# Issue order of the opening phase: pieces of the last chunk as they land, idle matmuls dropped, one v block loaded ahead of half of w_out, and new written-out orders for the first seventeen blocks

## The chip, the core and the metric

The kernel runs on one core of a Trainium2 chip. The metric is the device time of one execution in microseconds (us), the median over several runs. In profiles, PE is TensorE (matmuls), PEld its weight loads, DVE is VectorE, ACT is ScalarE, POOL is GpSimd, SP is SyncE; POOL, SP and ACT also issue DMAs.

## The reference

Cross-covariance attention over four batches, whose result goes through a two-layer MLP with a tanh GELU:

```
B, N, C = 4, 6080, 256
qn = q / (norm(q, axis=1) + 1e-6)          # columns over the 6080 tokens
kn = k / (norm(k, axis=1) + 1e-6)
s  = kn.transpose(0, 2, 1) @ qn / tau      # 256 x 256 for each batch
a  = softmax(s, axis=-1)
x  = (v @ a).reshape(24320, 256)
h  = x @ w_in                              # 256 -> 2048
g  = 0.5*h*(1 + tanh(sqrt(2/pi)*(h + 0.044715*h**3)))
out = g @ w_out                            # 2048 -> 256, float32
```

## The kernel before, in words

**Per batch.** The kernel never forms x. For each batch it sums the Gram matrix of q and k over the tokens (tile `G`) and the squares of their columns (tiles `ss`), makes the scores, their exponentials `eT` and row sums, and multiplies the attention matrix into w_in: `aw` = a·w_in, 256x2048 in bf16. The MLP then needs only v, transposed: h = v·aw.

**Per block.** The 24320 tokens are 48 blocks of 512 (the twelfth of each batch has 448). The transposed v of a block is the tile `vT`. For blocks 0 and 1, v comes into SBUF and TensorE transposes it (`load_v0`, `pe_vt`, copies by VectorE). From block 2 on, `cast_v(n)` has GpSimd issue a DMA that casts v to bf16 in DRAM (tile `vb`, line 152), and SyncE issues a transposing DMA from there (`load_vt`, line 162). A block's 16 column groups of h are made in 8 pairs. Pair p of block n is `g<p>`: four 512-wide matmuls into a two-bank PSUM tile, followed by ScalarE's GELU, `G<p>`. There are two such PSUM tiles, tags "h" and "b": in blocks 0 and 1, pairs 0, 2, 4, 6 use "h" and pairs 1, 3, 5, 7 use "b" (`SIDE`). A pair can only start when the GELU that reads the same tile is done. From block 2 on some pairs are made in sets by a scheme with fewer multiplications (`w0...`, `w1...`: matmuls `m1` to `m7`, ScalarE copies `cq`, `y5`, VectorE additions `ap`, `ax`, GELUs `Gq`, `Gr`, `Gx`).

**The second layer** is made by seven products per block, each in halves of four 256-wide matmuls (`M1A`, `M1B`, ... `M7B`). They read sums of g made by VectorE (`T1a` to `T4b`) and combinations of w_out (tile `wcomb`). Those combinations are prepared once, from the two halves of w_out (tiles `wst`, 1 MB each, `load_wout(0)` and `load_wout(1)`): `pA11` and `pS3` need the first half only, `pF0` is their first sum of both halves (line 660), `pS1`, `pF1`, `pS2`, `pS4` follow it. `M1` needs `pA11`, `M5` needs `pS1`, `M6` needs `pS2`. Results are turned by VectorE (`c11` to `c22`) and stored by SyncE's DMAs, four for a block.

**The opening.** Batch 0's q and k come in six chunks. The last chunk of 8 rows comes in five pieces, in the order q 0:4, k 0:5, k 5:8, q 4:6, q 6:8 (`PIECES`, tile `last`). For it, `square_rows` squares pieces on ScalarE (q 0:4) and VectorE (the others), `gram_row` adds Gram rows, `ss_rows(c, 1)` adds k's squares (256-wide matmuls against ones, line 274) and `ss_rows(c, 0)` adds q's (one-column matmuls, line 268). `warm(n)` issues n matmuls on zeros whose result nobody reads (line 369). `scores(0)` takes the sums to `eT`: logarithm and exponential on ScalarE for k's row factors (`lnk`, `rk`) and q's (`lnq`, `rq`), two products on VectorE (`S`), two exponentials on ScalarE. `first_aw` makes the first 512 columns of `aw`; the others are `aw2` to `aw7` (two 512-wide matmuls each, line 460) with a copy by VectorE (`ac2` to `ac7`, line 473). Pairs 2 and 3 need `ac2` and `ac3`; `aw6` writes the PSUM bank that `ac4` reads.

**Order.** Each engine runs its instructions in the order in which the program issues them. From block 0 on that order is written out by hand as strings of step names: `ORDER[WINDOW[n]]` lists the steps issued in the stretch of block n, and `x+1` or `x-1` is step x of the next or the previous block. `lt`, `lv`, `lq`, `lk` are DMA issues (`vT`, `vb`, q and k of a later batch). GpSimd's DMAs rotate over eight semaphores, so each waits until the eighth one before it has landed.

Of the kernel before, what the change touches and what calls it, by code (L numbers as in the profile page):

```python
# [18 lines left out]
def kernel(  # L19
# [962 lines left out]
    """g0 w0cq T3b-1 lt+2 w0y5 lv+3 row1-1 c11a-2 M4A-2 G0 T2b-1 w0m6 M5B-1 w0ap row3-1 ksq-1
    M4B-2 T2a-1 w0m2 w0m7 row0-1 w0ax w0m3 g3 w0Gq c21-2 lq+1 T3a-1 M5A-1 G3 M1B-1 T4a-1 M1A-1
    c22-2 w0Gx g4 SW1-2 y5-1 cq-1 g5 c11-2 G4 lt+3 lv+4 vs+1 w0m4 M6B-1 w0Gr M6A-1 qsq-1 g6
    ap-1 T1a lk+1 M3A-1 G6 row2-1 M3B-1 f1-1 w0m1+1 G5 M7A-1 T4b-1 w0m5+1 M7B-1 w0y5+1 c12-1
    row5-1 row3 ax-1 w0cq+1 row2 T2a row4-1 g7 ksq f2-1 w0m6+1 row0 w0ap+1 M4B-1 G7 M2A-1
    M2B-1 qsq M4A-1 c11a-1""",
    """g0 f3-2 c21-2 w0m7 G0 w0m2 T2b-1 w0m3 M5A-1 w0ax M1A-1 w0Gq T3a-1 g3 vs+1 w0Gx M1B-1 G3
    w0m4 f1-1 lq+1 M5B-1 g4 cq-1 c22-2 w0Gr w1m5 T1a G4 M6B-1 M6A-1 lt+3 lv+4 w1m1 y5-1 row1-1
    f2-1 w1cq g7 ap-1 w1y5 T4b-1 w1m6 G7 row5-1 w1ap M3A-1 lk+1 row4-1 T3b-1 M3B-1 qsq w0m5+1  # L990
    c12-1 w1m7 w1m2 w1ax w1m3 M7B-1 w1Gq T4a-1 M2A-1 w1m4 c11-2 M2B-1 w1Gr T2a M7A-1 w0y5+1
    row0 ax-1 w0m1+1 w1Gx""",
    """g0 c11a-2 w0cq T3b-1 M4A-2 G0 T3a-1 row5-1 w0m6 M4B-2 f3-2 ksq-1 row2-1 w0ap g3 c21-2
    T2b-1 w0m3 G3 w0m7 w0m2 w0ax M5B-1 lq+1 M1A-1 w0Gq T4a-1 M1B-1 f4-2 w0m4 cq-1 M5A-1 w0Gr
    f1-1 w1m5 M6A-1 y5-1 w1m1 M6B-1 f2-1 w1cq lt+3 lv+4 g4 ap-1 w1y5 c22-2 w0Gx w1m6 c11-2
    M3B-1 w1ap G4 M7B-1 vs+1 row3-1 M3A-1 qsq lk+1 w1m7 f3-1 g7 w1ax T4b-1 w1m3 G7 row4-1 w1m2
    c12-1 w1m4 row1-1 f4-1 M7A-1 w1Gr row2 w1Gq ax-1 M2A-1 T1a w0m1+1 w0m5+1 M2B-1 w0y5+1""",
    """g0 T2a-1 w0cq w1Gx-1 M4A-2 c11a-2 T4a-1 w0m6 G0 M4B-2 w0ap M5A-1 ksq-1 M5B-1 c22-2 c21-2
    row1-1 w0m2 vs+1 w0m7 w0m3 g3 w0Gq w0ax lq+1 T2b-1 M1B-1 G3 w0m4 c11-2 M1A-1 T3a-1 g4 w0Gr
    f1-1 cq-1 w1m5 G4 row4-1 M6A-1 lt+3 lv+4 T4b-1 w1m1 M6B-1 f2-1 y5-1 w1cq g7 ap-1 w1y5  # L1000
    T3b-1 w1m6 G7 M3A-1 w1ap lk+1 M3B-1 M7B-1 w0Gx c12-1 w1m7 ksq M7A-1 w1ax w1m3 w0m5+1 ax-1
    w1m2 w1m4 T1a M2A-1 w1Gr M2B-1 w1Gq row4 c11a-1 row3-1 w0m1+1 f3-1 row0-1 w0cq+1 M4B-1
    c11-1 M4A-1 w0y5+1 row5-1 qsq c21-1 w0m6+1""",
    """g0 w0ap f4-2 M5A-1 w1Gx-1 w0m3 c22-2 w0m7 G0 w0m2 w0ax row2-1 M1A-1 w0Gq T3a-1 M1B-1 w0m4
    T2a-1 g3 cq-1 T3b-1 w0Gr lq+1 M5B-1 G3 f1-1 g4 T2b-1 row0-1 G4 w1m1 M6A-1 T4a-1 w1m5 f2-1
    M6B-1 lt+3 lv+4 y5-1 w1cq g7 ap-1 w1y5 f3-1 w1m6 w0Gx row1-1 w1ap M3B-1 G7 M3A-1 vs+1 lk+1
    w1m7 w1m2 ksq row5-1 w1ax M7B-1 M7A-1 c12-1 T1a w1m3 w1m4 M2A-1 w1Gr M2B-1 ax-1 w1Gq
    w0m5+1 T4b-1 row3-1 w0m1+1 row1 c11a-1 w0cq+1 row0""",
    """g0 T2a-1 w0y5 c11-2 w1Gx-1 w0m6 M4B-2 w0ap G0 M4A-2 f4-2 row4-1 w0m3 qsq-1 w0m7 c22-2 g3
    w0ax w0m2 c21-2 G3 M5A-1 T2b-1 lq+1 w0m4 M1A-1 f1-1 w0Gr row3-1 M1B-1 w0Gq T4a-1 row5-1  # L1010
    w1m1 w1m5 T4b-1 cq-1 M5B-1 w1cq g4 f2-1 lt+3 lv+4 w1y5 T3a-1 w1m6 y5-1 M6A-1 G4 w1ap
    row2-1 M6B-1 f3-1 w0Gx w1m2 T3b-1 w1m3 w1m7 qsq lk+1 g7 ap-1 w1ax M7A-1 f4-1 G7 M3B-1 vs+1
    w1m4 M3A-1 w1Gr M7B-1 c12-1 w1Gq row1 ax-1 w0m5+1 w0m1+1 T1a M2A-1 w0cq+1 M2B-1 w1Gx""",
    """g0 c22-2 w0y5 c11a-2 row2-1 T3a-1 G0 w0m6 M4B-2 w0ap M5B-1 ksq-1 T2b-1 M4A-2 w0m7 c21-2 g3
    w0ax M1A-1 f1-1 G3 w0m2 w0m4 M1B-1 T2a-1 w0Gr w0m3 M5A-1 f2-1 cq-1 T3b-1 row4-1 w0Gq w1m5
    w1m1 c11-2 M6B-1 T4b-1 y5-1 M6A-1 w0Gx lt+3 lv+4 g4 ap-1 w1cq T4a-1 w1y5 M3A-1 f3-1 G4
    w1m6 M3B-1 w1ap row3-1 M7A-1 qsq c12-1 w1m3 vs+1 M7B-1 g7 ax-1 ksq T1a row4 row0 w1m7
    M4A-1 w1ax M2A-1 G7 f4-1 M2B-1 w1m4 c11a-1 row5-1 w1Gr w1m2 f1 M4B-1 w1Gq row1 row2 row0-1
    f2 row5 w0m5+1 f3 w0m1+1 T3a""",
    """lq+4 g0 w0cq c21-2 w0y5 M5B-1 T2a-1 G0 w0m6 M1A-1 w0ap M1B-1 w1Gx-1 f4-1 row3-1 w0m7 cq-1  # L1020
    g3 T2b-1 gc w0ax w0m3 G3 w0m2 M5A-1 T4a-1 w0m4 ss c11-2 w0Gr T3b-1 w0Gq w1m5 sv M6A-1
    T4b-1 pow w1m1 y5-1 M6B-1 c22-2 w1cq g4 lt+3 lv+4 ap-1 w1y5 vs+1 w1m6 G4 M7A-1 w1ap lk+4
    M7B-1 kf M3A-1 w0Gx ax-1 g7 kr T1a w1m7 G7 M3B-1 w1m3 c12-1 w1m2 krp w1ax w1Gq M4A-1 S1+1
    w0m5+1 w1m4 S0+1 w1Gx M2A-1 T2a w1Gr M2B-1 T3a w0y5+1 M4B-1 w0m1+1 th0+1 c21-1""",
    """g0 w0cq c22-2 c11a-2 th1 M1B-1 T3b-1 G0 M1A-1 T2b-1 w0m6 M5A-1 dn w0ap g3 cq-1 rc0 w0m7 G3
    w0m3 w0m2 w0ax M6B-1 lq+4 M5B-1 rc1 w0Gq w1m5 w0m4 M6A-1 rc2 w0Gr g4 y5-1 lt+3 lv+4 w1y5
    ap-1 w1m1 rc3 M3B-1 w1cq M3A-1 G4 vs+1 w1m6 M7B-1 w1ap w0Gx g7 c12-1 eT w1m7 G7 M2A-1 w1ax
    w1m3 w1m2 M7A-1 T4b-1 w1Gq M2B-1 T4a-1 lk+4 w1m4 rsum+1 ax-1 w0m5+1 w1Gr""",
    """g0 rs T1a-1 w0y5 w0m1 aw0 w0cq M4B-2 ac0 G0 M4A-2 c11-3 w0m6 aw1 w1Gx-1 w0ap g3 ac1 c21-2
    T2b-1 w0m7 w0m3 G3 aw2 w0ax M1B-1 c11a-2 w0Gx w0m2 ac2 w0m4 M1A-1 w0Gr T3b-1 M5B-1 w0Gq  # L1030
    w1m5 T2a-1 aw3 w1m1 cq-1 M5A-1 ac3 lt+3 lv+4 w1cq g4 vs+1 y5-1 w1y5 aw4 SW0 G4 M6B-1 w1m6
    M6A-1 ac4 w1ap g7 lq+4 ap-1 T3a-1 w1m7 aw5 c22-2 w1m2 w1m3 ac5 w1ax M7B-1 G7 T1a M3B-1
    M3A-1 w1Gx w1m4 w0m5+1 c12-1 w1Gr M7A-1 c11-2 aw6 w1Gq T4b-1 w0m1+1 M2B-1 ax-1 w0y5+1
    T4a-1 M2A-1 w0cq+1""",
    """g0 T2b-1 ac6-1 c11a-2 w0m6 G0 M4A-2 w0ap M4B-2 c22-2 aw7-1 c21-2 w0m7 g3 ac7-1 w0ax M1A-1
    G3 M1B-1 SW1-1 lk+3 w0m4 w0m2 cq-1 w0m3 T3b-1 M5A-1 w0Gr T2a-1 M6B-1 w0Gq M5B-1 vs+1 w1m1
    w1m5 y5-1 M6A-1 T3a-1 lt+3 lv+4 w1cq g4 ap-1 w1y5 T4a-1 w0Gx w1m6 M3B-1 w1ap G4 M7A-1
    M3A-1 c11-2 w1m2 c12-1 w1m3 w1m7 w1Gq g7 w1ax M7B-1 G7 w1m4 ax-1 M2A-1 T4b-1 M2B-1 w1Gr
    M4A-1 T1a w1Gx M4B-1 w0m5+1 w0m1+1 w0y5+1""",
    """g0 lq+3 c21-2 T3a-1 w0cq M1A-1 c11a-2 G0 T2a-1 w0m6 M1B-1 c22-2 M5A-1 ksq w0ap g3 T3b-1  # L1040
    w0m7 cq-1 row2 w0ax G3 row1 M5B-1 T2b-1 row3 w0m4 y5-1 w0m2 T4a-1 w0Gr w0m3 M6A-1 w0Gq
    c11-2 w1m5 w1m1 lt+3 lv+4 row4 M6B-1 w1cq g4 ap-1 w1y5 lk+3 T4b-1 w0Gx w1m6 M3A-1 G4 w1ap
    M7B-1 T1a M3B-1 qsq M7A-1 w1m2 ax-1 w1m3 w1m7 g7 w1Gq w1ax vs+1 M4B-1 G7 w1m4""",
    """g0 T2a-1 w1Gr-1 c22-2 M4A-2 w1Gx-1 c12-2 w0m5 T4a-1 w0m1 w0y5 M2B-2 c21-2 M2A-2 w0cq T3a-1
    row1 G0 row5 T3b-1 M1B-1 w0m6 c11a-2 M1A-1 ksq w0ap g3 lq+3 f1-1 w0m7 cq-1 M5B-1 w0ax G3
    row3 w0m3 T2b-1 w0m2 M5A-1 w0Gq row0-1 w0m4 lt+3 lv+4 M6B-1 w0Gr M6A-1 y5-1 w1m5 w1m1 w0Gx
    ap-1 g4 w1cq T4b-1 w1y5 M3A-1 vs+1 w1m6 G4 M7B-1 w1ap M3B-1 qsq f2-1 M7A-1 c11-2 w1m7 g7
    w1ax ax-1 row5-1 lk+3 G7 row0 f3-1 w1m4 w1m2 w1m3 c12-1 M4B-1 w1Gr c22-1 w0m5+1 f1 w1Gq
    M4A-1 w0m1+1 M2B-1 w0cq+1 f2 M2A-1 c21-1 w0y5+1""",
    """g0 T1a-1 w1Gx-1 w0m6 G0 M1A-1 w0ap M1B-1 c11a-2 row5 qsq w0m7 T2a-1 row1 g3 w0ax cq-1 w0m2  # L1050
# [171 lines left out]
```

## Time and profile before

| | |
|---|---|
| median of 5 runs (lowest to highest) | 698.01 us (697.73 to 698.22) |
| the profiled execution: its time / its span | 698.22 us / 696.4 us |
| PE, DVE, ACT, POOL busy, of the span | 96%, 90%, 89%, 10% |
| granted TensorE clock, mean | 0.997 |
| PE, its share of the chain that ended last | 92% |
| PE's first matmul / last wait for an input chunk ends / first matmul of block 0's pairs | 10.39 / 28.76 / 38.51 us |

The span runs from the first to the last instruction; the time is 1.82 us more. Times in the profile count from the span's start. A group line gives start, length, engine, source line, operation, output and inputs, and how many instructions are merged; the brackets give the idle time just before and what ended it. Ends of matmuls are modelled, and adjacent ones overlap; the time from one start to the next is what one takes of PE.

### The profile page before, as it was taken

How to read it: one execution, taken by the hardware profiler on the slowest of the kernel's cores; microseconds unless marked ns; L12 is line 12 of the kernel's file. 1: busy time of each engine (PE TensorE's matmuls, PEld its weight loads, DVE VectorE, ACT ScalarE, POOL GpSimd, SP SyncE). 2: the span in 40 equal slices, each digit the busy share in tenths (PEclk: the TensorE clock that was granted, in tenths of full speed). 3: DMA queues.
4: the chain of work that ended last, by engine and by line, in shares of the span. 5: the costliest groups of instructions: out<-in, count | busy, mean ns of one | idle time of the engine just before them, and what ended most of it. 6: DMA issues, size and time to landing. Idle time of an engine off the chain costs nothing.

```text
span 696.4 us, 14330 instructions
## 1 busy us (share of the span) xinstructions
...
## 2 busy tenths in 40 slices
...
DMA packets 161733, 79.33 MB, mean 114 GB/s; under 512 B 149472, under 2 KB 152672, under 8 KB 160672
## 3 DMA queue, kind: packets, MB, share of 16 engines
...
q14 instruction: 26, 0.21, 0.1%
...
## 4 chain that ended last, share of the span: by engine, by line
PE 92%; DMA 4%; DVE 2%; issue 1%; ACT 1%; POOL 0%; DVEq 0%; ACTq 0%; POOLq 0%
PE r L725 23%; PE h L520 21%; PE p L725 17%; PE rb L596 13%; PE qp L596 10%; PE G L247 5%; DMA t<-in_k_dram 3%; PE awp L460 2%; DMA t<-in_q_dram 1%; PE ss L281 0%; DVE xw L620 0%; PE ss L274 0%; PE warm L369 0%; DVE qp L617 0%; PE rk L405 0%
## 5 line engine op out<-in xcount | busy, mean ns | idle before, releaser
L725 PEld LDWEIGHTS <-wcomb 128*128 128x128 bf16 x2688 | 262.4, 98 | 42.7 <-issue 0.2
L530 ACT ACTIVATE g<-h 128x1024 bf16<-128x1024 f32 (+1 forms) x178 | 179.7, 1014 | 16.2 <-PE h L520 14.9
L725 PE MATMUL r<-t,wcomb 128*128 128x256 bf16 (+1 forms) x1152 | 164.6, 271 | 0.1
L520 PE MATMUL h<-vT,aw 128*128 128x512 bf16 (+1 forms) x582 | 159.5, 376 | 3.5
L622 ACT ACTIVATE g<-qp 128x1024 bf16<-128x1024 f32 (+1 forms) x103 | 104.6, 1015 | 5.8 <-PE qp L596 3.9
L725 PE MATMUL p<-g,wcomb 128*128 128x256 bf16 (+1 forms) x760 | 106.7, 271 | 0.0
L520 PEld LDWEIGHTS <-aw 128*128 128x128 bf16 x712 | 69.3, 98 | 49.0 <-issue 0.7
L596 PEld LDWEIGHTS <-sw 128*128 128x128 bf16 x824 | 80.2, 98 | 27.5 <-issue 0.9
L192 ACT ACTIVATE sq<-t 128x1536 bf16<-128x1536 bf16 (+4 forms) x59 | 79.4, 1359 | 7.4 <-DMA t<-in_q_dram 7.4
L617 DVE TENSOR_TENSOR qp<-rb,yw 128x512 f32<-128x512 f32 (+1 forms) x103 | 71.0, 689 | 12.7 <-PE rb L596 8.8
L596 PE MATMUL rb<-tv,sw 128*128 128x256 bf16 (+1 forms) x412 | 77.9, 271 | 0.4 <-DVE qp L617 0.2
L620 DVE TENSOR_TENSOR xw<-rb,yw 128x512 f32<-128x512 f32 (+1 forms) x103 | 69.6, 676 | 4.9 <-PE rb L596 4.0
L596 PEld LDWEIGHTS <-aw 128*128 128x128 bf16 x618 | 60.4, 98 | 12.9 <-issue 1.4
L612 ACT ACTIVATE qp<-rb 128x512 f32<-128x512 f32 (+1 forms) x103 | 59.7, 580 | 10.4 <-PE rb L596 5.8
L630 ACT ACTIVATE g<-xw 128x512 bf16<-128x512 f32 (+1 forms) x103 | 63.4, 625 | 1.6 <-DVE xw L620 1.5
L615 ACT ACTIVATE yw<-qp 128x512 f32<-128x512 f32 (+1 forms) x103 | 61.2, 594 | 3.9 <-PE qp L596 2.1
L627 ACT ACTIVATE g<-rb 128x512 bf16<-128x512 f32 (+1 forms) x103 | 61.1, 596 | 3.8 <-PE rb L596 2.6
L698 DVE TENSOR_TENSOR t<-g,t 128x1024 bf16<-128x1024 bf16 (+1 forms) x96 | 63.7, 667 | 0.6
L700 DVE TENSOR_TENSOR t<-g 128x1024 bf16<-128x1024 bf16 (+1 forms) x96 | 63.9, 673 | 0.0
L702 DVE TENSOR_TENSOR t<-t,g 128x1024 bf16<-128x1024 bf16 (+1 forms) x96 | 63.5, 670 | 0.0
L247 PE MATMUL G<-t 128*128 128x256 bf16 (+1 forms) x352 | 58.1, 273 | 1.7 <-DMA t<-in_k_dram 1.7
L686 DVE TENSOR_TENSOR t<-g 128x2048 bf16<-128x2048 bf16 (+1 forms) x48 | 57.5, 1197 | 0.1
...
## 6 DMA issues: line engine op xcount, KB each, us to landing
...
vb<-in_v_dram POOLq DMA_DIRECT2D x42, 256.0 KB, 4.4
...
wst<-in_moe_w_out_dram POOLq DMA_DIRECT2D x2, 1024.0 KB, 10.4
...
t<-in_k_dram POOLq DMA_DIRECT2D x3, 512.0 KB, 16.9
...
```

What stands on the lines that cost most here:

```text
L192: nc.scalar.activation(o, t[:np_, r, :], AF.Square)
L247: nc.tensor.matmul(G[b][:, jc, :], lhsT=qt[:np_, r, jc * 128 : jc * 128 + 128], rhs=kt[:np_, r, :], start=first and jc == 0, stop=jc == 1, ...
L520: mm = nc.tensor.matmul(hp[:, u, :cols], lhsT=AW[b][:, cc, fc * 128 : fc * 128 + 128], rhs=vt_tiles[n][:, cc, :cols], start=cc == 0, stop= ...
L530: nc.scalar.activation(gs(n)[:, 2 * p : 2 * p + 2, :cols], HP.pop((n, p))[:, :, :cols], AF.Gelu_apprx_tanh)
L596: GATE[0] = nc.tensor.matmul(acc[:, u * hc : u * hc + hc], lhsT=lhs[:, u * 128 : u * 128 + 128], rhs=rhs, start=m in (1, 5) and u == 0, st ...
L617: nc.vector.tensor_add(qp(n, i)[:, 1, :c], RB[n, i][:, :c], YW[n, i][:, :c])
L620: nc.vector.tensor_add(XW[n, i][:, :c], RB[n, i][:, :c], YW.pop((n, i))[:, :c])
L622: nc.scalar.activation(gs(n)[:, 2 * pa : 2 * pa + 2, :c].rearrange("p u (t x) -> p t u x", t=2), QP.pop((n, i))[:, :, :c].rearrange("p t ( ...
L698: nc.vector.tensor_sub(o, quarter(n, 1, 1, f0, f1), ts[1][:, f0:f1, :hc])
L700: nc.vector.tensor_sub(o, quarter(n, 1, 1, f0, f1), quarter(n, 0, 1, f0, f1))
L702: nc.vector.tensor_sub(o, ts[2][:, f0:f1, :hc], quarter(n, 1, 0, f0, f1))
L725: nc.tensor.matmul(ACCS[n, acc][:, :hc], lhsT=wcomb[:, w, fc, :], rhs=x, start=first and k == 0, stop=k == 3, skip_group_check=True)
```

## The change

In the opening, the six idle matmuls ahead of the last chunk go (the sixth entry of `WARM`). The first four Gram rows of the last chunk are issued ahead of q's sums of its first piece, k's sums of rows 5 to 7 ahead of the Gram rows 4 and 5. On GpSimd's queue the DMA for v of block 2 is issued ahead of that for the second half of w_out.

The orders of blocks 0 to 16 are written anew: the same steps, in another order. From block 17 on every block has the order that it had (`WINDOW` gives blocks 27 and 28 entries of their own, with the old text). TensorE's stream is shorter by the six idle matmuls and their weight loads and otherwise holds the same instructions.

```diff
-        WARM = [0, 4, 8, 8, 10, 6]
+        WARM = [0, 4, 8, 8, 10]
...
         c = nch - 1
         ss_rows(c - 1, 1)
         ss_rows(c - 1, 0)
-        warm(WARM[c])
         square_rows(c, 0, 0, 4, "act")
-        ss_rows(c, 0, range(0, 4))
         square_rows(c, 1, 0, 5, "dve")
         for i in range(4):
             gram_row(0, c, i)
+        ss_rows(c, 0, range(0, 4))
         ss_rows(c, 1, range(0, 5))
         square_rows(c, 1, 5, 8, "dve")
         square_rows(c, 0, 4, 6, "dve")
+        ss_rows(c, 1, range(5, 8))
         for i in (4, 5):
             gram_row(0, c, i)
-        ss_rows(c, 1, range(5, 8))
         ss_rows(c, 0, range(4, 6))
...
         load_wout(0)
         load_v0(1)
+        cast_v(2)
         load_wout(1)
-        cast_v(2)
         warm(8)
...
 ORDER = [
-    """g0 lt+2 lv+3 aw3 G0 aw2 ac3 g1 ac2 aw5 G1 aw4 lq+1 ac5 g2 SW0 g3 G2 ac4 aw7 G3 aw6 ac7 g4
-    ac6 g5 T1a G4 lk+1 vtp G5 g6 vtc0 pA11 g7 G6 vtc1 T2a M1A G7""",
-    """g0 pF0-1 lt+2 lv+3 M1B-1 G0 g1 pS1-1 pF1-1 G1 M5A-1 M5B-1 cq-1 g2 pS2-1 lq+1 T2b-1 g3 G2
-    pS4-1 M6A-1 G3 M6B-1 g4 pS3-1 y5-1 g5 G4 ap-1 T1a M3A-1 G5 w0m1+1 M3B-1 lk+1 T3b-1 g6
-    pA12-1 vs+1 g7 G6 c12-1 T3a-1 M7B-1 G7 M2B-1 T4a-1 M2A-1 T4b-1 pNA-1 M7A-1 w0m5+1 ax-1""",
+    """g0 lt+2 lv+3 aw3 G0 g1 ac3 aw2 G1 aw5 ac2 aw4 ac5 lq+1 g3 SW0 g2 G3 ac4 aw7 G2 aw6 ac7 g5
+    ac6 g4 G5 lk+1 vtp G4 pA11 g7 vtc0 g6 vtc1 G7 T1a G6 g1+1 T3a T2a""",
+    """g0 G1 pF0-1 lt+2 lv+3 M1A-1 G0 g3 pS1-1 M1B-1 G3 pF1-1 M5B-1 M5A-1 cq-1 g5 pA12-1 T2b-1
+    lq+1 pS2-1 g2 y5-1 G5 pS3-1 M6A-1 w0m1+1 G2 M6B-1 T3b-1 g7 ap-1 pNA-1 T4b-1 M7B-1 pS4-1 g4
+    G7 M7A-1 G4 vs+1 M3A-1 lk+1 M3B-1 ax-1 w0m5+1 T4a-1 g6 w0cq+1 c12-1 w0y5+1 M4B-1 G6 w0m6+1
+    M2A-1 w0ap+1 M2B-1 qsq M4A-1 c11a-1 row3 T1a row0""",
...
```

More of the change, by code (lines that the diff above doesn't have):

```diff
@@ L972 @@
     0, 1, 2, 3, 4, 5, 6, 7, 8, 9, 10, 11, 12, 13, 14, 15, 16, 17, 18, 19, 20, 21, 22, 23,
-    24, 25, 26, 15, 16, 17, 18, 19, 20, 27, 28, 29, 30, 31, 32, 33, 34, 35, 36, 36, 37,
-    38, 39, 40,
+    24, 25, 26, 27, 28, 17, 18, 19, 20, 29, 30, 31, 32, 33, 34, 35, 36, 37, 38, 38, 39,
+    40, 41, 42,
 ]
 ORDER = [
-    """g0 lt+2 lv+3 aw3 G0 aw2 ac3 g1 ac2 aw5 G1 aw4 lq+1 ac5 g2 SW0 g3 G2 ac4 aw7 G3 aw6 ac7 g4
-    ac6 g5 T1a G4 lk+1 vtp G5 g6 vtc0 pA11 g7 G6 vtc1 T2a M1A G7""",
-    """g0 pF0-1 lt+2 lv+3 M1B-1 G0 g1 pS1-1 pF1-1 G1 M5A-1 M5B-1 cq-1 g2 pS2-1 lq+1 T2b-1 g3 G2
@@ L980 @@
-    pS4-1 M6A-1 G3 M6B-1 g4 pS3-1 y5-1 g5 G4 ap-1 T1a M3A-1 G5 w0m1+1 M3B-1 lk+1 T3b-1 g6
-    pA12-1 vs+1 g7 G6 c12-1 T3a-1 M7B-1 G7 M2B-1 T4a-1 M2A-1 T4b-1 pNA-1 M7A-1 w0m5+1 ax-1""",
[L982 to L1050, printed above, removed]
-    T4a-1 G3 w0m3 M5A-1 c11-2 w0m4 T2b-1 row0 w0Gr M5B-1 f3-1 w1m5 w0Gq T3a-1 M6B-1 w1m1 T4b-1
-    M6A-1 lt+3 lv+4 w1cq row4-1 g4 y5-1 w1y5 ap-1 lq+3 row2-1 w0Gx w1m6 M7A-1 G4 w1ap M3A-1
@@ L1053 @@
-    T3b-1 M3B-1 ksq w1m3 c12-1 w1m2 w1m7 g7 w1ax w1Gq f4-1 M2A-1 w1m4 G7 vs+1 M2B-1 M7B-1
-    c11a-1 w1Gr""",
-    """g0 ax-2 w1Gx-1 T1a-1 w0m5 G0 M4A-2 w0m1 M4B-2 T2a-1 w0y5 row5 g3 c21-2 w0cq T3a-1 lk+2 qsq
-    row2-1 w0m6 M1B-1 w0ap M1A-1 G3 T2b-1 row3-1 w0m7 w0m3 w0ax w0m2 row4-1 w0Gq M5A-1 c22-2
-    w0m4 f1-1 M5B-1 w0Gr w1m5 g4 lt+3 lv+4 vs+1 cq-1 y5-1 w1y5 T3b-1 w1m1 row4 w1cq row1 f2-1
-    M6A-1 G4 c11-2 row2 w1m6 row0 w1ap M6B-1 w0Gx g7 ap-1 ksq T4a-1 w1m7 M3B-1 w1ax M3A-1 G7
-    w1m3 c12-1 w1m2 w1m4 T1a lq+3 M7A-1 w1Gr M2A-1 w1Gq M7B-1 f3-1 w0m5+1 T4b-1 w0m1+1 w0y5+1
@@ L1060 @@
-    M2B-1 ax-1""",
+    """g0 lt+2 lv+3 aw3 G0 g1 ac3 aw2 G1 aw5 ac2 aw4 ac5 lq+1 g3 SW0 g2 G3 ac4 aw7 G2 aw6 ac7 g5
[4 more added lines that the diff above has]
+    M2A-1 w0ap+1 M2B-1 qsq M4A-1 c11a-1 row3 T1a row0""",
@@ new lines @@
+    """g0 lt+2 lv+3 c21-2 row2-1 G0 w0m2 T2a-1 w0m3 M5B-1 T4a-1 M1A-1 w0Gq M1B-1 SW1-2 w0m7 cq-1
+    g3 qsq w0ax lq+1 M5A-1 T2b-1 g4 T3a-1 G3 c22-2 w0m4 M6A-1 y5-1 M6B-1 G4 g5 lt+3 lv+4 ap-1
+    T4b-1 w0Gx row1-1 M3B-1 w0Gr vs+1 M3A-1 G5 g6 c12-1 lk+1 T3b-1 ksq-1 row4 g7 T1a M7A-1 G6
+    f1-1 M7B-1 row5-1 G7 w0m1+1 row4-1 f2-1 w0m5+1 ax-1 M2A-1 w0cq+1 T2b M2B-1 w0y5+1""",
+    """g0 c22-2 ksq-1 c11-3 M4A-2 c11a-2 w0m6 M4B-2 w0ap G0 M5A-1 c21-2 row5-1 w0m2 f3-2 w0m3
+    w0m7 w0Gq g3 vs+1 w0ax M1A-1 lq+1 G3 M1B-1 T2a-1 w0m4 g4 cq-1 T4a-1 w0Gx T3a-1 M5B-1 w0Gr
@@ new lines @@
+    w1m5 G4 c11-2 M6B-1 lt+3 lv+4 T1a w1m1 row1-1 y5-1 M6A-1 w1y5 g7 T3b-1 w1cq ap-1 row3-1 G7
+    row0-1 w1m6 lk+1 M7B-1 w1ap M7A-1 ksq T4b-1 w0m5+1 w1m7 w1m2 w1ax w1m3 row2-1 w1Gq M3A-1
+    ax-1 w1m4 f1-1 M3B-1 w1Gr M4B-1 c12-1 w1Gx row4 M4A-1 f2-1 w0y5+1 w0m1+1 f3-1""",
+    """g0 c21-2 w0cq f4-2 qsq-1 M2A-2 w0m6 M2B-2 w0ap M1B-1 G0 T3b-1 M1A-1 w0m7 c11a-2 w0m2 w0m3
+    w0ax row2-1 w0Gq g3 c22-2 lq+1 T3a-1 w0m4 G3 M5B-1 T2b-1 g4 vs+1 cq-1 w0Gr M5A-1 T2a-1
+    M6B-1 G4 T4b-1 w1m1 lt+3 lv+4 w1m5 M6A-1 y5-1 T4a-1 w1cq g7 ap-1 w1y5 w1m6 w0Gx M7B-1 w1ap
@@ new lines @@
+    qsq M7A-1 lk+1 f1-1 row1 M3B-1 w1m7 ax-1 G7 w1m2 M3A-1 w1ax row1-1 row3-1 c11-2 w1Gx w1m3
+    c12-1 w1m4 M4A-1 f2-1 w1Gr T1a M4B-1 w1Gq w0m5+1 row5-1 w0m1+1 M2B-1 c21-1 w0cq+1 f3-1
+    M2A-1 w0y5+1 T2a row0-1 w0m6+1 ksq row5 w0ap+1""",
+    """g0 c11a-2 row3-1 G0 w0m2 w0m7 w0m3 w0ax row0-1 M5A-1 w0Gq f4-2 g3 T2b-1 M1B-1 G3 f1-1
+    M1A-1 lq+1 w0m4 g4 vs+1 w0Gr cq-1 w1m5 T3a-1 G4 w1m1 M5B-1 c22-2 M6A-1 c11-2 lt+3 lv+4
+    w1cq row4-1 f2-1 M6B-1 w1y5 T4b-1 w1m6 y5-1 g7 w1ap w0Gx ap-1 row2-1 row2 ksq T3b-1 lk+1
@@ new lines @@
+    w1m2 w1m7 M3B-1 w1ax M3A-1 G7 T4a-1 w1m3 w1m4 M7A-1 c12-1 w1Gr M7B-1 T1a w1Gq M2B-1 w0m1+1
+    w0m5+1 ax-1 M2A-1 w0cq+1 T3a""",
+    """g0 w1Gx-1 c11a-2 w0y5 M4A-2 T2b-1 row0-1 G0 w0m6 T2a-1 M4B-2 M5A-1 c22-2 qsq-1 c21-2 g3
+    f3-2 w0ap M1A-1 f4-2 M1B-1 lq+1 w0m7 cq-1 M5B-1 w0ax G3 row3-1 M6B-1 T4b-1 M6A-1 y5-1
+    T4a-1 w0m2 w0Gx w0m4 row4-1 ap-1 w0Gr row1-1 T3b-1 w1m5 lt+3 lv+4 w0m3 w1y5 row5-1 c11-2
+    w1m1 M3B-1 f1-1 w1cq M3A-1 w0Gq M7B-1 vs+1 w1m6 M7A-1 lk+1 w1ap g4 ksq ax-1 c12-1 w1m7
@@ new lines @@
+    w1m2 f2-1 M4B-1 G4 w1ax M4A-1 w1m3 w1Gx c21-1 M2A-1 f3-1 g7 w1Gq f4-1 w1m4 T1a G7 M2B-1""",
+    """g0 w1Gr-1 T2a-1 M1A-1 G0 w0m5 c11a-2 w0m1 T4a-1 row3-1 M1B-1 w0cq T3b-1 M5B-1 w0y5 row5-1
+    T2b-1 cq-1 w0m6 row0-1 qsq-1 g3 w0ap c11-2 lq+1 row2-1 T3a-1 w0m7 G3 M5A-1 c22-2 w0m2 w0ax
+    w0m3 M6A-1 w0Gq T4b-1 M6B-1 w0m4 vs+1 w1m5 y5-1 row1-1 lt+3 lv+4 w0Gr g4 ap-1 w0Gx f1-1
+    w1m1 G4 M7A-1 M3B-1 f2-1 M7B-1 w1cq lk+1 M3A-1 w1y5 w1m6 c12-1 qsq g7 w1ap M2B-1 ax-1 w1m7
+    G7 c22-1 w1m3 w1m2 w1ax M4A-1 w1Gq T1a M4B-1 w1m4 w0m5+1 w1Gr M2A-1 c21-1 row2 w0y5+1
@@ new lines @@
+    c11a-1 row4-1 row4 T3a w0m1+1 M5B w0cq+1 f3-1 M1A T2a w1Gx M1B ksq f4-1 w0m6+1 row3 M5A
+    w0ap+1""",
+    """g0 c11-2 cq-1 T2b-1 y5-1 w0m7 G0 w0m2 w0ax w0m3 M6A-1 T3b-1 M6B-1 w0Gq g3 ap-1 f1-1 w0Gx
+    w0m4 G3 g4 vs+1 M7B-1 w0Gr T4a-1 M7A-1 G4 f2-1 w1m5 row1-1 ax-1 w1m1 M3B-1 T1a w1cq row5-1
+    M3A-1 lt+3 lv+4 w1y5 w1m6 qsq g7 w1ap c22-1 M4A-1 c12-1 w1m7 ksq row5 w1ax w1m2 row0 row3
+    T4b-1 M2A-1 w1m3 f3-1 G7 row2 w1m4 f4-1 M4B-1 M2B-1 w1Gr c21-1 w0m5+1 w1Gq c11a-1 row0-1
+    M1B f1 row4 w0m1+1 row1 w0cq+1""",
@@ new lines @@
+    """g0 lq+4 f2-1 c11-2 w0y5 f3-1 M5B-1 T2a-1 G0 w0m6 M1A-1 w0ap M5A-1 gc T3a-1 g3 cq-1 w1Gx-1
+    f4-1 w0m3 w0m2 T2b-1 w0m7 w0Gq ss w0ax M6B-1 T4a-1 y5-1 G3 M6A-1 sv w0m4 pow ap-1 g4 w0Gr
+    T3b-1 w1m5 T4b-1 G4 M3B-1 lt+3 lv+4 w1m1 vs+1 M3A-1 w1cq M7A-1 kf w1y5 lk+4 w1m6 c12-1 g7
+    w0Gx w1ap kr M7B-1 T1a G7 w1m7 w1m2 w1m3 krp w1ax w1Gq M2B-1 ax-1 w0m5+1 S0+1 M2A-1 w1Gx
+    S1+1 w1m4 th0+1 M4A-1 c11a-1 w1Gr T3a M4B-1 th1+1 M5A c21-1 dn+1 w0m1+1 T2b""",
+    """g0 w0cq rc0 w0y5 w0m6 M1B-1 G0 w0ap M5B-1 M1A-1 rc1 y5-1 w0m3 cq-1 w0m7 w0m2 T2a-1 g3 w0Gq
```

46 lines of the change are left out of this document (added).

## The prediction

> **What bounds the kernel.** I read the page first: PE holds 92% of the chain that ended last. Then the stretches, to see where PE is not full:
>
> ```profile
> PE 92%; DMA 4%; DVE 2%; issue 1%; ACT 1%; POOL 0%; DVEq 0%; ACTq 0%; POOLq 0%
> ```
> ```profile
> 42.00:46.00 4.00, 4.00 (x20) 1.83 (x19) 3.72 (x9) 2.64 (x4) 0.13 (x1) 1.00 1.25 355
> 46.00:50.00 4.00, 3.95 (x28) 2.30 (x27) 3.93 (x6) 3.53 (x5) 0.53 (x1) 1.00 0.92 188
> ```
>
> The first figures after each window are its length and PE's busy time; the last three are clock, DMA share and GB/s. From 38.5 us on PE lacks 0.05 us here and there, which is also what one missing matmul record leaves. Its waits from 36 us to 280 us sum to 0.4 us (0.2 on `aw`, 0.2 on `xw`). So after 38.51 PE is full at clock 1.00, and the same matmuls in another order cannot end much sooner: the new orders have about half a microsecond to gain and any amount to lose. What else can be gained lies before 38.51. There I read the chain in order of time:
>
> ```profile
> 31.92 0.68 PE warm L369 x6
> 32.60 0.18 PE ss L268 x8
> 32.77 0.90 PE G L247 x8
> 33.67 0.55 PE ss L274 x5
> ...
> 35.59 0.90 PE warm L369 x8
> 36.49 0.46 PE vt_ps L324 x8
> 36.95 0.02 issue
> 36.98 0.76 DVE vT_pe L330 x2
> 37.73 0.14 DVE rs L353
> ...
> 38.51 0.39 PE h L520
> ```
>
> PE runs unbroken from 28.76 to 36.95, then VectorE copies the transposed v, takes the reciprocal of the row sums and writes `aw`. The six idle matmuls lie on this chain.
>
> **The opening.** Dropping `warm` x6 removes 0.68 us, if no wait takes its place. PE is at the last chunk at 31.92 then. By the instructions' waits the pieces landed at: k 0:5 by 31.57 (its square starts), k 5:8 at 15.62 + 16.9 = 32.52, q 4:6 by about 33.2, q 6:8 by 33.76 (its square waited for it). Laid end to end with the lengths above, PE comes to Gram rows 0 to 3 at 31.92, q's sums at 32.82, k's at 33.00 and 33.55 (their squares, at 0.82 and 0.49 us on DVE, are done near 32.4 and 33.1), Gram 4 and 5 at 33.88, q's sums at 34.32, Gram 6 and 7 at 34.40. Each is later than its piece, by 0.35 us (k 0:5), 0.7 (q 4:6), 0.6 (q 6:8). So PE keeps running, the sums end at 34.93, `warm(8)` at 35.83, the transposes of v at 36.29 (v landed at 23.27 + 11.8 = 35.07): all 0.66 earlier. k's sums now end 1.1 us earlier, at 33.88, but that is not what counts. ScalarE's four small steps and the exponentials would end at 36.5 instead of 37.40, 0.9 earlier, and then the copies of `vT_pe` stand ahead of `rs` in VectorE's queue and move only with PE: 36.32, `rs` at 37.03, first pair at 37.85. The gain is **0.66 us**. The second piece of w_in (29.01 + 7.5 = 36.5) is needed at 36.85, so it holds, by 0.3. The granted clock reads 1.00 in every stretch from 28.76 on, and PE gets no gap here that could change it.
>
> **v of block 2 ahead of w_out's second half.** GpSimd issued the second half at 36.15 after 0.76 us of waiting, and vb of block 2 at 37.04. Read by single issues, the DMA view gives the landings:
>
> ```profile
> wst<-in_moe_w_out_dram POOLq DMA_DIRECT2D x1, 1024.0 KB, 11.2
> vb<-in_v_dram POOLq DMA_DIRECT2D x1, 256.0 KB, 11.4
> ```
>
> That is 36.15 + 11.2 = 47.35 and 37.04 + 11.4 = 48.44; v of block 1, just ahead, landed at 34.62 + 9.8 = 44.42. The transfers follow each other: 2.93 us for wst, 1.09 for vb. The wait before 36.15 was for the last sums, which read the buffer (35.59, plus the queue's own lag); vb has no such wait and goes at 35.4, right after v; wst still goes near 36.2. So vb lands at 45.5, and SP's transposing DMA, at the head of its queue, starts there and not at 48.47, landing 6.1 later, at 51.6; the first step that reads it, `w0m1+1`, now comes near 54.6 (56.72 before). That is worth nothing by itself, but the new order needs it: landing at 54.57, as before, would be a tie. GpSimd's next issue (vb of block 3) waits for PE anyway. The cost is on wst: 44.42 + 1.09 + 2.93 = 48.44 at the old rate. VectorE needs it at `pF0`, which by its queue comes at 49.5 (copies of vT to 47.2, `T1a` 1.13, `T3a` 0.60, `T2a` 0.60); PE needs `pS1`, 1.99 after `pF0` starts (1.25 + 0.69 + 0.05), at `M5B`, about 51.96. So wst has until 49.9. Cover: 1.45 us.
>
> The trace has no wst beside a transposing DMA. Nearest rows: with vT of block 2 in flight (48.47 to 54.57), q and k of 384 KB landed 1.92 and 1.89 us apart, while 320 KB of k took 1.52 at 31 us, so no slowing; but vb of block 4 took 5.4 us (53.46 to 58.84) beside vT of block 3 where 1.09 is usual, five times. I take the first row, since wst like q and k goes into SBUF with 1 KB rows, and keep the second as a bound. The Trainium skill ("DMA: Bandwidth & Descriptors", section "Queues, rings and completion order") says that each DMA engine takes turns between queues that have work, packet by packet; by an estimate from that rule wst would go at half rate from 45.5 and land at 51.4, 1.5 us late, and the sum would be 699.5. The rows for q and k do not show that half rate.
>
> **The new orders.** From block 17 on nothing changes, and blocks 0 to 16 have the same steps, so PE's work is equal; only waits differ. The place to look is where the distance between steps shrank. Rows for it:
>
> ```profile
> 40.02 1.41 DVE L473 TENSOR_SCALAR aw<-awp,rs 128x512 bf16<-128x512 f32 x2 [0.77 <-PE awp L460]
> 43.34 0.75 DVE L473 TENSOR_SCALAR aw<-awp,rs 128x512 bf16<-128x512 f32 x1
> ```
> ```profile
> 47.81 1.94 ACT L530 ACTIVATE g<-h 128x1024 bf16<-128x1024 f32 x2 [0.24 <-PE h L520]
> ```
> ```profile
> 46.74 1.69 PE L520 MATMUL h<-vT_pe,aw 128*128 128x512 bf16 x7
> 48.48 0.60 PE L725 MATMUL r<-g,wcomb 128*128 128x256 bf16 x4
> 48.92 1.03 PE L520 MATMUL h<-vT_pe,aw 128*128 128x512 bf16 x4
> ```
>
> A pair takes PE 0.865; its GELU starts 0.21 after the pair (`g6` ends at 47.60, GELU 47.81), lasts 1.02 (0.92 when the next follows), and PE can use the tile 0.04 later. So two pairs on one PSUM tile must start 2.14 apart. A copy `ac` starts 0.20 after its matmuls and lasts 0.75. In the clock of before (first pair at 38.51), end to end:
>
> - `g0` 38.51, `aw3` 39.39, `g1` 39.82, `aw2` 40.69, `aw5`, `aw4`, then `g3` at 41.98. It needs `ac2`: 41.12 + 0.20 + 0.75 + 0.04 = 42.11. Wait 0.13. (Before, `aw2` stood ahead of `g1`.)
> - `aw6` at 44.27 needs `ac4`: `ac2` 41.32, `ac5` 0.66 on, `SW0` 0.66 on, `ac4` 0.93 on, end 44.32 + 0.04. Wait 0.09.
> - `g6` at 47.82 needs the GELU of `g4`, behind that of `g5`: wait 0.03.
> - `g1+1` now follows `g7`, `g6` at once, on the tile of `g7`. `g7` starts at 46.96, so the tile is free at 49.09; PE is there at 48.72. Wait 0.37. Before, `M1A`, `g0`, `M1B` lay between. Behind it on PE's queue is all of block 1.
> - `g0` of block 1 at 49.96 needs the GELU of `g6` (48.95 + 1.02 + 0.04): wait 0.05.
>
> Sum 0.67 us: what the opening wins is given back by 50 us. In block 1 I found no further wait: `g1+1` to `g3+1` are 2.17 apart, `M7B` needs `ap` 6.5 us after `pF0` starts, at 56.1 against 56.5. For blocks 2 to 16 I compared the distances on PE, block by block, with the same lengths: before has one shortage (0.17, at `w1m5` of block 9's stretch), after has two (0.07 and 0.08, in those of blocks 9 and 10), so nothing net. Apart from vT of block 2 (3 us of room), vT, q and k are wanted at least 4 us after they would land, the tightest being block 2's q, squared near 66 instead of 76.5. SyncE's reordered queue puts vT of block 5 ahead of block 0's stores and block 1's stores ahead of vT of block 6, which is wanted some 25 us later.
>
> **Sum.** 698.22 - 0.66 + 0.67 = 698.2 for the profiled execution, which lay 0.21 above the median: **698.0 us**.
>
> **Rivals.**
> 1. *The waits of the new order do not come*, because ScalarE or VectorE release PE sooner than these rows say, or because PE's waits fill time that it would lose later. Then the 0.66 stays: 697.4. For it: the distances miss by only 0.03 to 0.37. Against it: the 2.14 for one tile is made of three rows that hardly vary.
> 2. *w_out's second half is late* (slower). Place: `pF0` on VectorE, then `M5B` on PE, with all of both queues behind. It decides at a landing of 49.9; beyond that each microsecond costs one. A landing at 51.9 (2.9 us of transfer turned into 6.4) gives 700.0; five times slower, as vb of block 4, some 708. For it: that row. Against it: q's and k's rows, and that half of it is in before the transposing DMA is under way.
> 3. *The opening does not speed up*, because a piece lands later than read or the second piece of w_in does (cover 0.3): the block's waits stay, 698.7.
>
> **How the numbers follow.** Forecast 0.50, rival 1 0.25, rival 2 0.13, rival 3 or more small waits in blocks 2 to 16 0.10 (a third of it beyond 699.4), and 0.02 for a gain of over 1.4, which would need more than the 0.66 and all of PE's 0.4 of waits. A measurement of this kernel tells about 0.2%, 1.4 us, from no change. So: faster 0.02, slower 0.16, same 0.82. The range goes from rival 1 with the 0.2 of waits that it might also spare, 697.2, to 699.4.
>
> **What would show it.** In the profile after: `warm` x8 near 34.9 and the first `h` near 37.85; vb's transposing DMA near 45.6; `pF0` near 49.5 without idle before it; PE idle by 0.3 to 0.4 ahead of the pair after `g6`, ended by ACT, near 48.1, and by 0.1 near 41.4; PE's other waits up to 280 us under half a microsecond. Wrong: no PE wait near 48; DVE idle at `pF0` on wst; PE waits of over 0.5 us anywhere in blocks 2 to 16.

## The result, and the profile after

| | before | changed |
|---|---|---|
| median (lowest to highest) | 698.00 us (697.73 to 698.79, 49 runs) | 700.39 us (697.7 to 706.16, 28 runs) |
| ratio, 95% interval | | 1.0042 [1.0029, 1.0056] |
| profiled execution: time / span | 698.22 / 696.4 us | 706.16 / 704.4 us |
| last of the six `rk` matmuls (line 405), less the first `h` | 503.7 - 38.51 = 465.19 us | 511.6 - 37.65 = 473.95 us |

The change makes the kernel slower, by 0.42%. The times of the changed kernel spread over 8 us from run to run, those of before over 1 us; the profiled execution is the slowest of its runs, so it shows the loss in full.

The last row of the table serves as a ruler below. Between the first `h` and the last `rk`, far behind the last block that has a new order, every kernel here does the same work on PE, and before does it with next to no wait; what goes beyond 465.19 us is lost on the way. The changed kernel starts its blocks 0.86 us earlier and loses 8.76.

The shares of the chain that ended last, from the page of the changed kernel: PE has 2 points less than before, DMA 3 more.

```profile
PE 90%; DMA 7%; issue 1%; DVE 0%; POOL 0%; ACT 0%; DVEq 0%; POOLq 0%; ACTq 0%
```

The same chain in order of time, around the place (start, length, what):

```profile
35.21 10.57 DMA vb<-in_v_dram
...
45.80 14.65 DMA vT<-vb
```

The copy of v of block 2 lands at 45.8 as the exchange wants it, and its transposing DMA starts at once. But it takes 14.65 us, where it took 6.1 before, and lands at 60.5: 6 us later than before, though it started 2.7 us earlier. PE's own rows, in the timeline of the changed kernel:

```profile
34.64 1.03 PE L369 MATMUL warm<-zeros_bf,ones_bf 128*128 128x256 bf16 x8
...
37.65 1.04 PE L520 MATMUL h<-vT_pe,aw 128*128 128x512 bf16 x3 [0.37 <-DVE aw L363]
...
48.24 1.94 PE L520 MATMUL h<-vT_pe,aw 128*128 128x512 bf16 x8 [0.45 <-DVE t L686]
...
60.49 0.58 PE L596 MATMUL rb<-vT,aw 128*128 128x256 bf16 x2 [5.53 <-DMA vT<-vb]
```

The opening gains, one small wait of the new order comes at 48.24, and then PE stands for 5.53 us on vT of block 2. That is not all that the late transfer costs. The stretches (length, PE, PEld, DVE, ACT and POOL busy, then granted clock, DMA share, GB/s):

```profile
50.00:55.00 5.00, 4.96 (x33) 3.12 (x32) 4.97 (x7) 4.72 (x8) 1.43 (x2) 1.00 1.32 85
55.00:60.00 5.00, 0.00 (x0) 0.00 (x0) 0.34 (x1) 1.81 (x2) 0.00 (x0) 0.84 1.28 65
60.00:65.00 5.00, 4.29 (x15) 2.31 (x16) 2.90 (x6) 1.02 (x1) 0.00 (x0) 0.50 1.13 189
```

The granted clock is 0.50 from about 58.4 us, while PE is idle, until 65.2 in the finer stretches. From 60.49 on, when PE works again, that is 4.7 us at half speed, by estimate some 2.35 us lost. 0.7 for the orders (shown below), 5.53 and 2.35 make 8.6 of the 8.76 us.

Where the transfer's time went is read from the DMA view of single microseconds. These are the two queues (packets, MB, time that packets took as a share of 16 engines) between 53 and 54 us: q1 is the transposing queue, which holds vT of block 2 and, issued some 49.8 us into the span, vT of block 3; q0 is the one with GpSimd's loads and copies. Before:

```profile
q1 hardware_dynamic: 840, 0.21, 118.1%
q0 software_dynamic: 1, 0.00, 0.1%
```

Changed:

```profile
q1 hardware_dynamic: 221, 0.06, 83.6%
q0 software_dynamic: 14, 0.04, 59.6%
```

Before, most of the packets move in a gap of the loads. In the changed kernel both queues have work, both are busy by their shares, and together they move 0.09 MB (0.06 and 0.04 are rounded) where either alone moves about 0.2 (0.21 for q1 above; 0.19 to 0.22 for q0 from 48 to 51 us before, where q1 has no packet). The page's stretches above say the same: 85 and 65 GB/s from 50 to 60 us, where before had 188 GB/s from 46 to 50.

### The profile page after: what moved, and what is told of

Read it like the earlier page. It is cut to its first block, busy times and chain, and to the rows that moved or that the text cites. A ratio compares the mean times of both kernels' runs of the same rounds, so it can differ in the third digit from the quotient of the medians.

```text
span 704.4 us, 14314 instructions
## 1 busy us (share of the span) xinstructions
PE 673.2 (96%) x5418; PEld 530.5 (75%) x5493; DVE 629.9 (89%) x1243; ACT 616.5 (88%) x894; POOL 73.0 (10%) x135
## 4 chain that ended last, share of the span: by engine, by line
PE 90%; DMA 7%; issue 1%; DVE 0%; POOL 0%; ACT 0%; DVEq 0%; POOLq 0%; ACTq 0%
PE r L725 23%; PE h L520 20%; PE p L725 17%; PE rb L596 13%; PE qp L596 10%; PE G L247 5%; DMA last<-in_k_dram 2%; DMA vT<-vb 2%; DMA vb<-in_v_dram 2%; PE awp L460 1%; DMA qk_f<-in_k_dram 1%; PE ss L281 0%; DVE qp L617 0%; DVE first L124 0%; PE rk L405 0%
```

## The experiments

The theories at the start. **A**: the exchange loses the time, by starting the transposing DMA of block 2 where it runs beside other transfers: the loads of q and k (**A1**) or the transposing DMA of block 3 (**A2**). **B**, the rival: the new orders bring the wait, with the exchange or without. The tables' last column is the ruler: what a profiled execution loses beyond the 465.19 us of before.

### Taking the change apart

`e1_after_again` is the changed kernel once more, to see whether the late transfer is a rule.

> The changed kernel again, for the spread of its times and a second trace. Theory A (the transposing DMA of block 2's v now runs beside w_out's second half and the loads queued behind it, and its flight time varies from run to run): times from 697.5 to 706, median near 700; in the trace the time of this execution above about 697.5 equals the wait of w0m1 of block 2 on vT plus the matmuls at half clock behind it. Theory B (the waits are spread over the new orders): the excess lies in many small waits of PE.

`e2_swap_undone` is the changed kernel with the two DMAs in the old sequence:

```diff
-        cast_v(2)
         load_wout(1)
+        cast_v(2)
```

> The changed kernel with only the two DMA issues put back (w_out's second half ahead of v of block 2). Theory A: the transposing DMA starts near 48 us again, lands near 54.5, w0m1 of block 2 wants it near 54.5: times 697.0 to 698.0, spread under 1 us. Theory B (the new order wants vT of block 2 too early, whatever the loads do): as slow as the changed kernel or slower, 699 to 706, since the DMA even starts 2.7 us later.

`e3_swap_only` is the kernel before with the opposite edit and nothing else.

> The kernel before with only the two DMA issues exchanged. Theory A: vT of block 2 is wanted at 56.7 us and lands between 51 and 60, so some executions wait up to 4 us plus matmuls at half clock: 698 to 703, a spread of several us. Theory B: 698.0 with no spread, since the order of before wants vT 2 us later.

`e4_head_only` is the kernel before with the opening's edits (`WARM`, the sequence of sums and Gram rows), in the old orders and without the exchange.

> The kernel before with only the opening's edits (six idle matmuls dropped, Gram rows and k's sums moved), the DMA issues and the orders of before. Both theories: the opening's gain alone, 0.66 to 0.86 us, so 697.1 to 697.4, spread 0.5 us; vT of block 2 lands at 54.5 and is wanted near 56.

| run | median (lowest to highest), us | ratio, 95% interval | transposing DMA of block 2: start, length | PE's wait for it | first `h` | lost |
|---|---|---|---|---|---|---|
| e1_after_again | 704.02 (697.81 to 705.16) | 1.0068 [1.0045, 1.0092] | 45.57, 14.8 | 5.5 | 37.56 | 7.75 |
| e2_swap_undone | 697.92 (697.59 to 698.38) | 1.0000 [0.9991, 1.0008] | 48.54, 6.1 | none | 37.48 | 0.73 |
| e3_swap_only | 703.76 (699.44 to 705.76) | 1.0077 [1.0056, 1.0098] | 45.46, 14.6 | 3.5 | 38.24 | 5.27 |
| e4_head_only | 698.50 (697.71 to 701.38) | 1.0009 [1.0001, 1.0017] | 48.28, 9.9 | 2.4 | 37.38 | 4.23 |

PE's waits between 30 and 280 us in the kernel with only the exchange (us in total, times, longest):

```profile
PE rb L596 <- DMA vT<-vb: 3.5, 1, 3.5
PE h L520 <- DVE aw L363: 0.2, 1, 0.2
```

The exchange alone brings the loss (703.76 us, more than the 698 to 703 expected), and without it the changed kernel stands where before stands: B falls. The new orders only add to the wait, 5.5 us instead of 3.5: there PE wants vT of block 2 at 54.96 and not at 56.60. The run without the exchange also weighs the forecast's other two terms against each other, since it starts its blocks 1.03 us earlier than before, loses 0.73 of it on the way, and ends level.

The opening alone was a surprise: seven of its twelve runs lie over 698.4. The profiled one shows the same fault in small, a transposing DMA of 9.9 us, though nothing in GpSimd's sequence was exchanged. Its row on PE:

```profile
58.19 0.38 PE L596 MATMUL rb<-vT,aw 128*128 128x256 bf16 x2 [2.44 <-DMA vT<-vb]
```

### Beside what is the transfer slow?

`e5_loads_late` is the changed kernel with two of the loads of q and k held back until vT of block 2 is in:

```diff
 block 0:
-    ... ac5 lq+1 g3 ... G5 lk+1 vtp ...
+    ... ac5 g3 ... G5 vtp ...
 block 1:
-    ... pA12-1 T2b-1 lq+1 pS2-1 ...
+    ... pA12-1 T2b-1 lq lk lq+1 pS2-1 ...
```

> The changed kernel with the q and k loads of the first later chunk issued only after the third-last pair of block 1's first half (near 53.5 us) instead of at 40 and 46 us. Theory A1 (the transposing DMA and the casting loads of q and k slow each other down whenever their packets overlap): vT of block 2 then has the queue to itself from about 49.8 us on and lands near 52, flight 6 to 7 us, no PE wait at w0m1; k's rows may wait near 62, so the time is 697.2 to 700. Theory A2 (two transposing DMAs in flight slow each other): vT of block 2 still lands near 60, PE waits 5 us, 703 to 705.

`e6_vt3_late` is the changed kernel with the transposing DMA of block 3 (`lt+2`) held back until PE has used vT of block 2 (`lg` is `lt` with that wait):

```diff
-    """g0 G1 pF0-1 lt+2 lv+3 ... w0m1+1 G2 ...
+    """g0 G1 pF0-1 lv+3 ... w0m1+1 lg+2 G2 ...
```

> The changed kernel with the transposing DMA of block 3 held back until block 2's vT has been used (w0m1), the loads as they were. Theory A1: vT of block 2 still flies 12 to 15 us beside q and k, PE waits 3 to 5.5 us, 701 to 705. Theory A2: vT of block 2 lands near 52, no wait, 697.2 to 698.

| run | median (lowest to highest), us | ratio, 95% interval | transposing DMA of block 2 | PE's wait for it | lost |
|---|---|---|---|---|---|
| e5_loads_late | 697.77 (697.67 to 698.36) | 0.9999 [0.9990, 1.0008] | 45.98, 5.0 | none | 0.77 |
| e6_vt3_late | 704.53 (703.08 to 705.58) | 1.0093 [1.0079, 1.0107] | 45.66, 12.7 | 3.5 | 7.16 |

The DMA view of the run with the loads held back, issues of 45.9 to 46.0 us, and its queues from 50 to 52 us (q0 is absent there):

```profile
vT<-vb SPq DMA_TRANSPOSE x1, 5.0
```
```profile
q1 hardware_dynamic: 960, 0.24, 52.3%
```

In `e6_vt3_late`, where only vT of block 2 is on the transposing queue, from 53 to 54 us:

```profile
q1 hardware_dynamic: 200, 0.05, 61.1%
q0 software_dynamic: 23, 0.06, 50.6%
```

With no load beside it the transfer takes 5.0 us and the loss is gone; with the other transposing DMA out of its way, and the loads still there, it is slow and late all the same, and both queues move as little. A1 holds and A2 falls as the main cause. This transfer is 2 us shorter than the changed kernel's; whether the other transposing DMA adds those 2 us, one profile of each doesn't tell. In the first of the two runs the transposing DMA of block 4 meets the loads instead and takes 12.8 us (55.71 to 68.51); nobody waits for it, as its data are wanted later. The slowdown goes with the meeting, not with the block.

### Getting the opening's gain without the meeting

Could the loads be moved ahead of the transposing DMA instead of behind it? `e7_head_early_loads` is `e4_head_only` with the load of k, `lk+1`, moved up and the copy of v of block 3 put behind it; `e8_new_order_early_loads` is `e2_swap_undone` with the same:

```diff
 block 0 of e7 (e8: in its own order, the same three steps):
-    """g0 lt+2 lv+3 aw3 G0 ... aw4 lq+1 ac5 ... G4 lk+1 vtp ...
+    """g0 lt+2 aw3 G0 ... aw4 lq+1 lk+1 lv+3 ac5 ... G4 vtp ...
```

> The kernel before with the opening's edits (as in the run of the opening alone) and with the v of block 3 put behind the q and k loads in the queue, both of these issued at 41 us. Theory A1: q and k land near 50.4 and 52.3 instead of 51.5 and 54, the transposing DMA of block 2 (packets from 51 on) overlaps them by 1.3 us less and lands by 54.6 in nearly every execution: 697.1 to 697.5, spread under 0.7 us. If overlap with the loads is not the cause, it spreads to 701 like the opening alone.

> The changed kernel with the two DMA issues put back and with v of block 3 behind the q and k loads, as in the run just above. Theory A1: as with the exchange undone, 697.6 to 698.0, since there vT of block 2 was in time already; the waits of the new order near 41, 43 and 48 us stay.

| run | median (lowest to highest), us | ratio, 95% interval | transposing DMA of block 2 | copy of v of block 4 issued | first `h` | lost |
|---|---|---|---|---|---|---|
| e7_head_early_loads | 699.68 (697.74 to 702.40) | 1.0027 [1.0014, 1.0040] | 48.20, 8.1 | 49.24 | 37.51 | 0.60 |
| e8_new_order_early_loads | 697.84 (697.50 to 698.55) | 0.9998 [0.9989, 1.0007] | 48.25, 6.0 | 50.33 | 37.49 | 0.72 |

The first missed. In its profiled execution, one of its best at 697.88, q and k had landed at 49.98 and 51.93, and still the transfer took 8.1 us, now beside the copies of v of blocks 3 and 4 (landed at 53.26 and 56.14). So beside copies from DRAM to DRAM it can be late too, but in another way than beside the loads. From 51 to 54 us q1 moved 1018 packets, of the 1056 that such a transfer has (the count of `e6_vt3_late` up to 58.5 us), and from 53 to 54 both queues together moved 0.39 MB, so no rate was lost there; the last 38 packets came by 55.8, and the landing waits for the last. That a copy held these up is argued from this one trace, not shown.

Side by side, the five kernels in which the second half of w_out goes first show a pattern: where the copy of v of block 4 is issued at 50.2 us or later (before, e2, e8) the times lie within 1.1 us; where it is issued near 49.1 or 49.2 (e4, e7) they spread. In the program it stands behind the first pair of block 1, so the opening's gain moves it forward, towards the gap that the transposing DMA had used. The microsecond of 53 to 54 in `e4_head_only`, to be held against those of before and of the changed kernel:

```profile
q1 hardware_dynamic: 23, 0.01, 133.3%
q0 software_dynamic: 1, 0.02, 14.2%
```

The copy has only one packet there, so the gap is not filled, and still the transposing queue moves 23 packets instead of 840. They are in flight for longer (133.3% of 16 engines, for so few); what holds them is not shown.

`e9_head_vb4_later` takes the pattern at its word: `e4_head_only` with that one copy moved back.

```diff
 block 1:
-    """g0 pF0-1 lt+2 lv+3 M1B-1 G0 g1 pS1-1 pF1-1 G1 M5A-1 ...
+    """g0 pF0-1 lt+2 M1B-1 G0 g1 pS1-1 pF1-1 G1 lv+3 M5A-1 ...
```

> The opening's edits alone, in the orders of before, with the copy of v of block 4 issued behind the second GELU of block 1 instead of behind its first pair (near 50.6 us instead of 49.1). Theory: with the opening's edits alone the times spread up to 701.4 because this copy moved forward by the opening's gain and took the gap in the loads' queue in which the transposing DMA of block 2 had moved its packets. Then its transfer here takes 6 us again in every execution, PE does not wait for vT of block 2, and the time is 698.0 less the opening's 0.7 to 0.9: 697.1 to 697.4, with no run above 698. Rival: the copy is not the cause (the loads of q and k alone, moved forward with the rest, are): runs up to 701 again, a median of 697.8 to 698.6, and in a slow run a transposing DMA of 9 to 10 us with a wait of PE of 2 us or more.

`e10_exchange_loads_behind` goes the other way: opening and exchange in the old orders, with copy and loads behind the transfer.

```diff
 block 0:
-    ... aw4 lq+1 ac5 ... G4 lk+1 vtp ...
+    ... aw4 ac5 ... G4 vtp ...
 block 1:
-    """g0 pF0-1 lt+2 lv+3 M1B-1 ... g2 pS2-1 lq+1 ...
+    """g0 pF0-1 lt+2 M1B-1 ... g2 lv+3 lq lk pS2-1 lq+1 ...
```

> The opening's edits and the exchange on GpSimd's queue, in the orders of before, with the copy of v of block 4 and the two loads of q and k of block 0 issued only behind pair 2 of block 1 (near 52 us). Theory: v of block 2 is then transposed between the second half of w_out and these loads with little beside it, in 5.0 to 6.5 us, and lands near 51 to 52; no wait of PE for it, no stretch at clock 0.5; the orders' waits of the changed kernel are absent, so the opening's gain stays: 697.0 to 697.5 and no run above 698. Rival: the later loads of q and k run beside the transposing DMAs of blocks 3 and 4, and these come late instead: PE waits of over 1 us for vT of block 3 or 4 between 60 and 72 us, and times of 699 or more.

| run | median (lowest to highest), us | ratio, 95% interval | transposing DMA of block 2 | first `h` | lost |
|---|---|---|---|---|---|
| e9_head_vb4_later | 697.09 (696.89 to 697.58) | 0.9989 [0.9980, 0.9998] | 48.64, 6.1 | 37.52 | 0 |
| e10_exchange_loads_behind | 697.78 (697.38 to 698.32) | 0.9999 [0.9990, 1.0008] | 45.27, 6.1 | 37.19 | 0.52 |

Moving one copy of 256 KB by 1.4 us (issued at 50.54 instead of 49.10) turns a kernel that spreads up to 701.4 into the fastest here, and one of the steadiest, 0.8 us below before. So the place of this copy is the cause of the opening's fault; how it acts is not shown. Its microsecond of 53 to 54 has the gap again:

```profile
q1 hardware_dynamic: 638, 0.16, 98.0%
q0 software_dynamic: 2, 0.00, 1.6%
```

The last kernel lost most of its gain (697.78 against 697.91 for before) in a way that the expectation had not named. VectorE's and PE's rows:

```profile
48.18 1.23 DVE L660 TENSOR_TENSOR wf<-wst,wst 128x1024 f32<-128x1024 f32 x1 [0.61 <-DMA wst<-in_moe_w_out_dram]
```
```profile
50.19 1.05 PE L725 MATMUL p<-t,wcomb 128*128 128x256 bf16 x8 [0.28 <-DVE wcomb L662]
```

In the old orders `pF0` is due at 47.6, and the second half of w_out lands at 48.2, since the exchange has put it behind the copy of v. It took 12.4 us from its issue, as in the changed kernel. By the starts on PE the wait costs 0.44 of the 0.52 us lost (48.89 to 50.19 for a pair that takes 0.865).

## Why the prediction was wrong

The forecast was no change, 698.0 in a range up to 699.4; the result is 700.39, slower. By its own steps:

**The opening: right.** Forecast 0.66 us, with `warm` x8 at 34.93 and the first `h` at 37.85; the profile has 34.64 and 37.65, 0.86 earlier than before. Part of this is chance, as the first `h` came at 38.24 in a run without these edits and between 37.19 and 37.74 in nine other kernels or runs with them. In time, the run `e9_head_vb4_later` has it nearly pure: 697.09 against 697.91 for before beside it, 0.8 us.

**The waits of the new orders: right.** Forecast 0.67 us; the ruler gives 0.73, 0.72 and 0.77 in the three runs with these orders and no late transfer. This is no luck of the sum: by the starts on PE in the changed kernel, `g3` loses 0.15 (forecast 0.13), `aw6` 0.07 (0.09), `g1+1` 0.40 (0.37) and `g0` of block 1 0.05 (0.05). The one wait of size, at `g1+1`, was put on a PSUM tile free 0.86 before 49.09, that is at 48.23: PE starts there at 48.24 (the 0.45 in its brackets is too long by one matmul that the records miss). The profile names VectorE's sum, which ends at 48.20, and not the GELU, which by its row of two (47.17 to 49.11) ends at about the same time.

**w_out's second half: right for this kernel.** Forecast to land at 48.44, it landed at 48.63, and `pF0` began at 49.32 without idle. The two did not overlap, since the transposing DMA's packets only started at 49.5, 3.7 us after its issue. So rival 2 did not come, but partly by luck: the row that the forecast chose for it was never put to the test. In `e10_exchange_loads_behind` VectorE did wait for this half, 0.61 us, but by its place in the queue and an earlier `pF0`, not by a slower transfer.

**vT of block 2: the step that failed.** "SP's transposing DMA ... starts there and not at 48.47, landing 6.1 later, at 51.6". It started there and landed 14.7 later. The 6.1 was a length from one place in the traffic, carried over to another as if it belonged to the instruction. It was long enough to break the 3 us of room by 5.5. The slowing was looked for on one side only: q and k landing 1.9 us apart beside that transfer was read as "no slowing", but the transfer's packets did not move before 51.3 us there, and the queue of the loads was nearly empty from 52 to 54. The row that did show an overlap, the copy of v of block 4 at five times its usual length, was kept as a bound for w_out and never turned round to ask what the transposing DMA itself would suffer. And a wait of PE was priced at its length; those of 2.44, 3.5 and 5.5 us here also cost the clock.

On the rule of the Trainium skill ("DMA: Bandwidth & Descriptors", section "Queues, rings and completion order") that a DMA engine takes turns between its queues: it points the right way, since overlap does slow both. By an estimate from it, however the turns divide, the sum would stay near the 0.2 MB in a microsecond that either queue moves alone. The rows show 0.09 and, from 54 to 55 us, 48 GB/s: beside the loads of q and k the two queues do not share the rate, they lose it.

What inside the DMA engines loses it stays open, and with it why the loads of q and k cost the rate and a copy in `e7_head_early_loads` did not. So does why the same program meets the loads fully in most executions and hardly in some (697.7 to 706.16 us); the traces show small shifts of all transfers between executions, and no run tells which of them decides.
